# Token sums taken from the banks of the first MoE's way out, over its features as 0, 2, 1, 3

## The chip, the cores and the metric

The kernel runs on one NeuronCore of a Trainium2 chip. The metric is the time of one execution in microseconds of the device. The core's engines are TensorE (PE in the rows, its weight loads PEld), VectorE (DVE), ScalarE (ACT), GpSimd (POOL) and SyncE (SP), which here only issues DMAs. TensorE has two levels of its clock, 1.2 and 2.4 GHz; a granted clock of 1.00 in the rows is the higher.

## The reference, cut to what matters

```python
def reference(**kwargs):
    attn_out = _attn_ref(q, k, v, proj)              # (2, 8, 768, 64), masked by hash buckets
    x = attn_out.transpose(0, 2, 1, 3).reshape(1536, 512)
    # first MoE: d_model 512, d_ff 768
    h = np.maximum(np.maximum(x @ w1, x @ w2), x @ w3)
    x = h @ w_out
    # second MoE: d_model 512, d_ff 2048
    h = x @ w_in
    g = h * (1.0 / (1.0 + np.exp(-1.702 * h)))
    return g @ w_out
```

The weights come as 64 bit floats, all else in 32 bit. The change concerns the step from `h @ w_out` of the first MoE to `x @ w_in` of the second.

## The kernel before, in words

All matrices are kept as a high part, rounded to the matmul's 32 bit format, and a low part, the rest; a product is three matmuls (high by high, high by low, low by high), each 128 by 128 by 512. Tokens lie along the free dimension, in `NCH` = 3 blocks `a` of 512; features along the partitions, in blocks of 128.

After the attention (to about 250 us) the first MoE's way in (`up1`) makes `h` in six blocks of d_ff, 54 units of 12 matmuls. Its way out (`down1`) goes over the four feature blocks `et` of 128 and the three token blocks `a`: 12 units of 18 matmuls. Each unit fills one bank of PSUM; ScalarE copies it to the high part `xh` (L641) and VectorE subtracts to get the low part `xl` (L642). This is the input `X[1]` of the second MoE.

The second MoE goes over the 2048 features of d_ff in eight rounds `p` of two blocks of 128 (`FG` = 2). In round 0 the way in is plain: six units `up2` of 12 matmuls (two feature blocks by three token blocks). From round 1 on the products of the two feature blocks with the first two token blocks are taken with seven products instead of eight (`seven`, a form of Strassen's scheme, on 2 by 2 blocks): each is 6 matmuls, and they need sums of weight blocks (`sums`: `shi`, `slo`, made by GpSimd and ScalarE from round to round) and four sums of token blocks T1 to T4 (`ts[0]` to `ts[3]`, tiles `th` and `tl`, made once). The third token block goes plain, in two units `up2`. The way out (`down2`) has 12 units of 6 matmuls a round, which are added up in `res`.

The token sums use blocks numbered by feature half and token block: for `c` = 0, 1 the block 11 is feature block `c` with tokens 0, 12 feature block `c` with tokens 1, 21 and 22 the same of feature block `c + 2`. T1 = 12 - 11, T2 = 22 - T1, T3 = 22 - 12, T4 = T2 - 21. `token_sums()` returns 16 steps. Each block is put together as `xh + xl` on VectorE (L689), subtracted on VectorE (L702), the result copied to the high part on ScalarE (`high`, L693) and subtracted to the low part (`low`, L696) on GpSimd (T1, T2) or VectorE (T3, T4). One step is issued after each unit of round 0: six in `up2`, ten in `down2`.

What fixes the order: `unit` calls a unit's function, then the work that the unit before put into `due` (so gelu's second half comes one unit late), then `after`, then `w_tick`, which lets every weight block in flight take its next step. Every engine goes through its instructions in the order in which they are issued (`in_order`). A weight block's steps are: raw load (two buffers, the next load is issued after L468), magnitude on ScalarE (L448), clamp on GpSimd (L452), three bit steps on VectorE (L460, L464, L468), cast to `whi` on ScalarE and `wlo` on GpSimd (L475, L495). gelu is a sigmoid on ScalarE (L666), a product on VectorE (L669), and the split `gh` and `gl` on ScalarE and GpSimd (L670, L671).

The memory pools lie on top of each other: `mo[0]` for the whole MoE part, `mo[2]` above it, first with the `h` of the first MoE (`sb_h`), then with what the second needs (`sb_g`). The banks are eight tiles `acc`.

Of the kernel before, what the change touches and what calls it, by code (L numbers as in the profile page):

```python
# [6 lines left out]
F32R = mybir.dt.float32r  # L7
# [4 lines left out]
ALU = mybir.AluOpType  # L12

P = 128
CH = 512
# [75 lines left out]
def build(tc, q, k, v, proj, w1, w2, w3, w_out, m2_in, m2_out, out):  # L91
    nc = tc.nc
# [5 lines left out]
    EC = E // P  # L98
# [18 lines left out]
    def st(shape, tag, bufs, dtype=F32, pool=None):  # L117
        seq[0] += 1
        if pool is None:
            pool = sb if tag in shared else at  # L120
        return pool.tile(shape, dtype, tag=tag, name=f"{tag}_{seq[0]}", bufs=bufs)
# [12 lines left out]
    def f32(ap):  # L134
        return ap.bitcast(F32)
# [163 lines left out]
    X = {}  # L299
# [100 lines left out]
    def w_block(key, src, n, tag):  # L400
        wplace[key] = len(wblocks)
        wblocks.append((src, n, tag))

    def w_out_group(n):
        for f in range(n * FG, (n + 1) * FG):
            w_block(("out", f), m2_out[f * P:(f + 1) * P, :].rearrange("p (c f) -> p c f", c=EC), EC, "wo")
# [2 lines left out]
        for i, w in enumerate((w1, w2, w3)):  # L409
            w_block(("up", ft, i), w[:, ft * P:(ft + 1) * P].rearrange("(c p) f -> p c f", p=P), EC, "w")  # L410
    w_out_group(0)
    for et in range(EC):
        for a in range(2):
            w_block(("down", et, a), w_out[a * 3 * P:(a + 1) * 3 * P, et * P:(et + 1) * P]
                    .rearrange("(c p) f -> p c f", p=P), 3, "w")
# [135 lines left out]
    def w_tick(start):  # L551

        for entry in list(wflight):
            i, steps = entry
            if i is not None and split_is_next(steps) and not w_free(i) or i is None and not sums_free():
                break
            step = steps.pop(0)
            if step:
                step()
            if not steps:  # L560
                wflight.remove(entry)
        i = wstate[1]
        if start and i < len(wblocks) and len(wflight) < (5 if wstage[0] else 3) and i in wraw and (mo[0] is not None or wblocks[i][2] == "w"):
            wflight.append((i, w_steps(i)))
            wstate[1] += 1
            wflight[-1][1].pop(0)()
            return True
        return False
# [6 lines left out]
    def w_get(*key):  # L575
        i = wplace[key]
        if i not in wsplit:
            raise RuntimeError(f"block {i} is used before it is split")
        return wsplit[i]
# [6 lines left out]
    mo = [None, None, None]  # L586
# [3 lines left out]
    def bank():  # L590
        seq[0] += 1
        return mo[1].tile([P, CH], F32, tag="acc", name=f"acc_{seq[0]}", bufs=8)
# [26 lines left out]
    def split1(ft, a):  # L619
        if a == 0:  # L620
            Hs[ft] = (st([P, NTOK], "hh", FT, F32R, mo[2]), st([P, NTOK], "hl", FT, F32R, mo[2]))
        hh, hl = Hs[ft]
        s = slice(a * CH, (a + 1) * CH)
        nc.scalar.copy(hh[:, s], hm[a])
        nc.gpsimd.tensor_tensor(out=hl[:, s], in0=hm[a], in1=f32(hh[:, s]), op=ALU.subtract)

    def down1(et, a):
        cur = [w_get("down", et, n) for n in range(2)]
        if not X.get(1):
            X[1] = (st([P, EC, NTOK], "xh", 1, F32R), st([P, EC, NTOK], "xl", 1, F32R))  # L630
        xh, xl = X[1]
        s = slice(a * CH, (a + 1) * CH)
        o = bank()
        for c in range(FT):
            (wh, wl), (hh, hl) = cur[c // 3], Hs[c]
            for z, (w, h) in enumerate(((wh, hh), (wh, hl), (wl, hh))):
                nc.tensor.matmul(o, w[:, c % 3, :], h[:, s], start=(c == 0 and z == 0),  # L637
                                 stop=(c == FT - 1 and z == 2))
        if a == NCH - 1:
            wdone.update(wplace["down", et, n] for n in range(2))  # L640
        nc.scalar.copy(xh[:, et, s], o)  # L641
        nc.vector.tensor_tensor(out=xl[:, et, s], in0=o, in1=f32(xh[:, et, s]), op=ALU.subtract)  # L642


    gs = {}
# [30 lines left out]
    ts = {}  # L676
    due = []

    def token_sums():

        xh, xl = X[1]
        steps = []
        for n in range(4):
            ts[n] = tuple(st([P, 2, CH], f"t{z}{n}", 1, F32R, mo[2]) for z in "hl")

        def block(c, half, a):
            t = st([P, CH], "hc", 4, pool=mo[0])
            s = slice(a * CH, (a + 1) * CH)
            nc.vector.tensor_tensor(out=t, in0=f32(xh[:, c + 2 * half, s]), in1=f32(xl[:, c + 2 * half, s]), op=ALU.add)  # L689
            return t  # L690

        def high(n, c, t):
            nc.scalar.copy(ts[n][0][:, c], t)  # L693

        def low(n, c, t, eng):
            eng.tensor_tensor(out=ts[n][1][:, c], in0=t, in1=f32(ts[n][0][:, c]), op=ALU.subtract)  # L696

        for c in range(2):
            got = {}

            def sub(to, x, y):
                nc.vector.tensor_tensor(out=to, in0=x, in1=y, op=ALU.subtract)  # L702

            def a(c=c, got=got):
                got["11"], got["12"] = block(c, 0, 0), block(c, 0, 1)

            def b(c=c, got=got):
                sub(got["11"], got["12"], got["11"])
                got["22"] = block(c, 1, 1)

            def d(c=c, got=got):
                high(0, c, got["11"])
                sub(got["12"], got["22"], got["12"])

            def e(c=c, got=got):
                low(0, c, got["11"], nc.gpsimd)
                high(2, c, got["12"])
                sub(got["22"], got["22"], got["11"])

            def f(c=c, got=got):  # L720
                low(2, c, got["12"], nc.vector)
                high(1, c, got["22"])
                got["21"] = block(c, 1, 0)

            def g(c=c, got=got):
                low(1, c, got["22"], nc.gpsimd)
                sub(got["21"], got["22"], got["21"])

            def h(c=c, got=got):
                high(3, c, got["21"])  # L730

            def i(c=c, got=got):
                low(3, c, got["21"], nc.vector)
            steps += [a, b, d, e, f, g, h, i]
        return steps

    def seven(p):

# [96 lines left out]
    if True:  # L835
# [89 lines left out]
        for j in range(2):  # L925
            for n in range(8):
                bits = n > 3
                name, a = "kq"[n // 2 % 2], n % 2
# [23 lines left out]
        for u in range(NU):  # L952
            hd, c = divmod(u, NTILE)
            g, j = divmod(hd, 2)
# [12 lines left out]
        for jq in range(NU // 2):  # L967
            hd, i = divmod(jq, 3)
            g, j = divmod(hd, 2)
# [55 lines left out]
        def unit(fn, *args, after=None, matmuls=12, target=None):  # L1025
            n = len(due)
            fn(*args)
            for _ in range(n):
                due.pop(0)()
            if after:  # L1030
                after()
            if target is not None:
                w_tick(wstate[1] < target)
                return
            owed[0] = min(owed[0] + matmuls / 12, 2 * PACE)
            for _ in range(2 if matmuls > 12 else 1):
                if w_tick(owed[0] >= PACE and wstate[1] < wplace["in", FG]):
                    owed[0] -= PACE
# [4 lines left out]
        for ft in range(1, FT):  # L1043
            for i in range(3):
                for a in range(NCH):
                    unit(up1, ft, i, a, bank, after=(lambda: split1(ft, a)) if i == 2 else None)
        for et in range(EC):
            for a in range(NCH):
                unit(down1, et, a, matmuls=3 * FT)
        sb_h.__exit__(None, None, None)  # L1050
        sb_g = tc.tile_pool(name="sb_g", bufs=1, reuse_waits="tile")
        mo[2] = sb_g.__enter__()
        steps = token_sums()
        wstage[0] = True

        def ahead():
            if steps:
                steps.pop(0)()

        for p in range(FT2 // FG):  # L1060

            nxt = wplace.get(("in", FG * (p + 1)), len(wblocks))
            if p == 0:
                for n in range(NCH * FG):
                    unit(up2, n % FG, n // FG, after=ahead, target=nxt + 1 + (n >= 2))
                    w_tick(False)
            else:
                while steps:
                    steps.pop(0)()
                for n, x in enumerate(seven(p)):  # L1070
                    unit(x, matmuls=6, target=nxt + 1 + (n >= 4))
                for f in range(FG):
                    unit(up2, FG * p + f, NCH - 1, target=nxt + 2)
            for t in range(B * NTILE):
                unit(down2, p, t, matmuls=6, after=ahead, target=nxt + 2 + (t >= 1) + (t >= 6))
# [34 lines left out]
```

## Time and profile before

| | us |
|---|---|
| time, median of 3 runs (lowest to highest) | 703.24 (702.67 to 703.45) |
| the profiled execution | 702.86 |
| its span, from the first to the last instruction | 701.1 |
| TensorE busy | 690.2 (98%) |
| VectorE busy | 535.1 (76%) |
| GpSimd busy | 452.3 (65%) |
| ScalarE busy | 372.0 (53%) |
| mean granted clock of TensorE | 0.995 |

Times in the rows count from the span's start. A matmul's duration in the rows reaches from its start to its modelled end and overlaps the next one, so the distance between starts is what it takes of the engine. Brackets behind an instruction show its engine's idle time before it and what ended it; `L` and a number is the line in the kernel.

### The profile page before, as it was taken

The numbers are of one execution on the slowest core, as the hardware profiler recorded it, in microseconds if no ns is written. First come the engines' busy times: TensorE is split into PE (matmuls) and PEld (weight loads), VectorE is DVE, ScalarE is ACT, GpSimd is POOL, SyncE is SP. The second block draws the span as 40 slices with busy tenths as digits, with TensorE's granted clock in tenths as the row PEclk, the third lists the DMA queues.
The fourth block names the chain that finished last, engine by engine and source line by source line (L and its number), as shares of the span: only waits on it lengthen the run. The fifth ranks groups of instructions, "written<-read, shape, count | busy, mean of one in ns | idle before, by whom it ended". The sixth has DMA issues, their size and how long they took to land.

```text
span 701.1 us, 10931 instructions
## 1 busy us (share of the span) xinstructions
PE 690.2 (98%) x3741; PEld 591.4 (84%) x3742; DVE 535.1 (76%) x928; ACT 372.0 (53%) x727; POOL 452.3 (65%) x488
## 2 busy tenths in 40 slices
PE   9999999999999999999999999997999999999998
PEld 5899999999999988888888888885888888888886
DVE  7999999999999736634555353889888878798864
ACT  4898898888889713332323222654443534344340
POOL 5487878798888844524543422585959687785950
PEclk9999999999999999999999999998999999999999
DMA  5657676777454103321212122002221121212104
GB/s 115 142 133 158 132 181 145 174 175 166 110 130 107 49 6 97 111 64 60 90 47 75 38 80 64 31 30 61 73 74 64 62 87 64 61 61 60 61 0 180
DMA packets 74406, 63.34 MB, mean 90 GB/s; under 512 B 41376, under 2 KB 65184, under 8 KB 74352
## 3 DMA queue, kind: packets, MB, share of 16 engines
q1 hardware_dynamic: 74128, 62.52, 34.2%
q8 instruction: 30, 0.49, 0.3%
q14 instruction: 24, 0.20, 0.1%
q10 hardware_dynamic: 224, 0.13, 0.1%
HBM read 38.80 MB, written 3.15 MB: 60 GB/s over the span
## 4 chain that ended last, share of the span: by engine, by line
PE 89%; DVE 6%; POOL 2%; issue 1%; DMA 1%; ACT 0%; SPq 0%; DVEq 0%; POOLq 0%; ACTq 0%
PE acc L604 20%; PE acc L814 16%; PE acc L790 9%; PE S L307 8%; PE PV L355 8%; PE T L337 8%; PE acc L637 7%; PE acc L655 6%; PE T L205 2%; PE T L178 1%; DVE se L314 1%; DVE ptl L347 1%; PE T L604 1%; DVE hc L702 1%; POOL wlo L495 0%
## 5 line engine op out<-in xcount | busy, mean ns | idle before, releaser
L671 POOL TENSOR_TENSOR gl<-hm,gh 128x512 fp32r<-128x512 f32 x48 | 74.4, 1573 | 49.7 <-ACT gh L670 49.7
L328 POOL TENSOR_SCALAR se<-se,rc 128x768 f32<-128x768 f32 x96 | 87.5, 924 | 24.3 <-DVE rc L325 8.9
L347 DVE TENSOR_TENSOR ptl<-T,pth 128x512 fp32r<-128x512 f32 x144 | 94.5, 682 | 3.6 <-ACT pth L343 3.5
L320 ACT ACTIVATE se<-se,mn 128x768 f32<-128x768 f32 x96 | 90.9, 947 | 5.3 <-DVE se L314 4.7
L314 DVE TENSOR_SCALAR_CACHE_REDUCE se<-S 128x768 f32<-128x768 f32 x96 | 90.9, 949 | 1.9 <-PE S L307 1.6
L307 PE MATMUL S<-kst,qst 128*128 128x512 f32 (+3 forms) x384 | 87.0, 350 | 0.0
L343 ACT CAST pth<-T 128x512 fp32r<-128x512 f32 x144 | 80.2, 588 | 12.6 <-PE T L337 10.6
L337 PE MATMUL T<-ident,se 128*128 128x128 f32 x576 | 80.4, 273 | 0.8 <-DVE ptl L347 0.6
L604 PE MATMUL acc<-xh,whi 128*128 128x512 f32 x204 | 79.4, 389 | 0.0
L604 PE MATMUL acc<-xl,whi 128*128 128x512 f32 x204 | 79.4, 389 | 0.0
L604 PE MATMUL acc<-xh,wlo 128*128 128x512 f32 x204 | 79.4, 389 | 0.0
L819 DVE TENSOR_TENSOR res<-acc,res 128x512 f32<-128x512 f32 (+1 forms) x85 | 57.3, 679 | 24.7 <-PE acc L814 24.5
L814 PE MATMUL acc<-wolo,gh 128*128 128x512 f32 (+1 forms) x194 | 75.0, 387 | 0.0
L814 PE MATMUL acc<-wohi,gh 128*128 128x512 f32 (+1 forms) x194 | 74.9, 387 | 0.0
L495 POOL TENSOR_TENSOR wlo<-wmag,whi 128x512 fp32r<-128x512 f32 (+1 forms) x42 | 56.6, 1348 | 28.3 <-ACT whi L475 28.3
L355 PE MATMUL PV<-pth,vst 128*128 128x256 f32 x288 | 74.5, 293 | 0.0
L448 ACT ACTIVATE wbits<-wraw 128x512 f32<-128x512 f32 (+1 forms) x58 | 37.9, 656 | 66.5 <-DMA wraw<-in_moe_w_dram 29.9
L452 POOL TENSOR_SCALAR wbits<-wbits 128x512 f32<-128x512 f32 (+1 forms) x58 | 40.4, 696 | 49.0 <-ACT wbits L448 48.6
L337 PEld LDWEIGHTS T<-ident,se 128*128 128x128 f32 x576 | 65.4, 140 | 5.9 <-DVE ptl L347 1.1
L355 PE MATMUL PV<-ptl,vst 128*128 128x256 f32 x288 | 70.2, 279 | 0.0
L614 DVE TENSOR_TENSOR hm<-acc,hm 128x512 f32<-128x512 f32 x34 | 23.5, 690 | 56.8 <-PE acc L604 54.5
L307 PEld LDWEIGHTS S<-kst,qst 76*128 76x128 f32 (+1 forms) x384 | 59.2, 190 | 5.3 <-DVE se L314 0.5
(159 smaller groups left out, 1635.3 us busy)
## 6 DMA issues: line engine op xcount, KB each, us to landing
wraw<-in_moe_w_dram SPq DMA_DIRECT2D x18, 512.0 KB
wraw<-in_moe_w_out_dram SPq DMA_DIRECT2D x16, 512.0 KB
wraw<-in_moe_w_in_dram SPq DMA_DIRECT2D x16, 512.0 KB
kst<-kq SPq DMA_DIRECT2D x42, 192.0 KB
qst<-kq SPq DMA_DIRECT2D x42, 192.0 KB
raw<-in_k_dram SPq DMA_DIRECT2D x16, 192.0 KB
raw<-in_q_dram SPq DMA_DIRECT2D x16, 192.0 KB
raw<-in_v_dram SPq DMA_DIRECT2D x16, 192.0 KB
```

Of the source, the lines that this page charges most:

```text
L307: nc.tensor.matmul(pss[:, x], qs[r, k, c * P:(c + 1) * P], ks[r, k, x], start=k == 0, stop=k == 1)
L314: nc.vector.tensor_scalar(out=se[u], in0=pss[:, :S], scalar1=1.0e9, scalar2=None, op0=ALU.min, op1=ALU.min, accum_out=mn[u])
L320: nc.scalar.activation(se[u], se[u], AF.Exp, bias=mn[u], scale=-1.0, accum_out=sm[u // 2][:, u % 2:u % 2 + 1])
L328: nc.gpsimd.tensor_scalar(out=se[u], in0=se[u], scalar1=rc[u // 2][:, u % 2:u % 2 + 1], scalar2=1.0, op0=ALU.mult, op1=ALU.mult)
L337: nc.tensor.transpose(pst[:, i * P:(i + 1) * P], se[2 * jq + o][:, c * P:(c + 1) * P], ident)
L343: nc.scalar.copy(ptr[jq][0][:, n * 512:(n + 1) * 512], tps[jq, n])
L347: nc.vector.tensor_tensor(out=ptr[jq][1][:, s], in0=tps[jq, n], in1=f32(ptr[jq][0][:, s]), op=ALU.subtract)
L355: nc.tensor.matmul(pv[jq], vs[:, c, :], ptr[jq][t].rearrange("p (o c n) -> p c o n", o=2, c=NTILE)[:, c], start=(c == 0 and t == 0), stop= ...
L604: nc.tensor.matmul(o, w[:, c, :], x[:, c, s], start=(c == 0 and z == 0), stop=(c == EC - 1 and z == 2))
L671: nc.gpsimd.tensor_tensor(out=gl, in0=g, in1=f32(gh), op=ALU.subtract)
L790: nc.tensor.matmul(o, w[:, c], x[:, c], start=n == 0, stop=n == len(turns) - 1)
L814: nc.tensor.matmul(o, g[:, s], w.rearrange("p c f -> p (c f)")[:, e], start=n == 0, stop=n == len(turns) - 1)
```

## The change

The way out goes over the feature blocks as 0, 2, 1, 3, and the weight blocks are listed in the same order. So the four blocks of `c` = 0 are done in its first half and those of `c` = 1 in its second. Each unit of `down1` now calls `token_sums(c, half, a, o)` with its bank `o`: the blocks 11 and 21 are copied out of the bank by ScalarE, T1 and T2 are subtractions of VectorE that read the bank, and one unit later (`rest`, in `due`) T3 and T4 follow as subtractions between tiles, and T1 and T3 are split. T2 and T4 are split in 8 steps that are issued after the units of round 0, one each. All low parts are made on GpSimd. The tiles of T1 and T3 are in `mo[0]`, those of T2 and T4 in `mo[2]`; two of the unsplit sums take the tag `hm0`, the others `hc`. The sums come from the bank's values instead of `xh + xl`.

```diff
--- before.py
+++ after.py
@@ -409,7 +409,9 @@
         for i, w in enumerate((w1, w2, w3)):
             w_block(("up", ft, i), w[:, ft * P:(ft + 1) * P].rearrange("(c p) f -> p c f", p=P), EC, "w")
     w_out_group(0)
-    for et in range(EC):
+
+    ETS = [c + half * EC // 2 for c in range(EC // 2) for half in range(2)]
+    for et in ETS:
         for a in range(2):
             w_block(("down", et, a), w_out[a * 3 * P:(a + 1) * 3 * P, et * P:(et + 1) * P]
                     .rearrange("(c p) f -> p c f", p=P), 3, "w")
@@ -640,6 +642,7 @@
             wdone.update(wplace["down", et, n] for n in range(2))
         nc.scalar.copy(xh[:, et, s], o)
         nc.vector.tensor_tensor(out=xl[:, et, s], in0=o, in1=f32(xh[:, et, s]), op=ALU.subtract)
+        due.append(token_sums(et % 2, et // 2, a, o))
 
 
     gs = {}
@@ -676,63 +679,44 @@
     ts = {}
     due = []
 
-    def token_sums():
-
-        xh, xl = X[1]
-        steps = []
-        for n in range(4):
-            ts[n] = tuple(st([P, 2, CH], f"t{z}{n}", 1, F32R, mo[2]) for z in "hl")
-
-        def block(c, half, a):
-            t = st([P, CH], "hc", 4, pool=mo[0])
-            s = slice(a * CH, (a + 1) * CH)
-            nc.vector.tensor_tensor(out=t, in0=f32(xh[:, c + 2 * half, s]), in1=f32(xl[:, c + 2 * half, s]), op=ALU.add)
-            return t
-
-        def high(n, c, t):
-            nc.scalar.copy(ts[n][0][:, c], t)
-
-        def low(n, c, t, eng):
-            eng.tensor_tensor(out=ts[n][1][:, c], in0=t, in1=f32(ts[n][0][:, c]), op=ALU.subtract)
-
-        for c in range(2):
-            got = {}
-
-            def sub(to, x, y):
-                nc.vector.tensor_tensor(out=to, in0=x, in1=y, op=ALU.subtract)
-
-            def a(c=c, got=got):
-                got["11"], got["12"] = block(c, 0, 0), block(c, 0, 1)
-
-            def b(c=c, got=got):
-                sub(got["11"], got["12"], got["11"])
-                got["22"] = block(c, 1, 1)
-
-            def d(c=c, got=got):
-                high(0, c, got["11"])
-                sub(got["12"], got["22"], got["12"])
-
-            def e(c=c, got=got):
-                low(0, c, got["11"], nc.gpsimd)
-                high(2, c, got["12"])
-                sub(got["22"], got["22"], got["11"])
-
-            def f(c=c, got=got):
-                low(2, c, got["12"], nc.vector)
-                high(1, c, got["22"])
-                got["21"] = block(c, 1, 0)
-
-            def g(c=c, got=got):
-                low(1, c, got["22"], nc.gpsimd)
-                sub(got["21"], got["22"], got["21"])
-
-            def h(c=c, got=got):
-                high(3, c, got["21"])
-
-            def i(c=c, got=got):
-                low(3, c, got["21"], nc.vector)
-            steps += [a, b, d, e, f, g, h, i]
-        return steps
+    td = {}
+
+    def t_high(n, c, t, pool):
+        if n not in ts:
+            ts[n] = tuple(st([P, 2, CH], f"t{z}{n}", 1, F32R, pool) for z in "hl")
+        nc.scalar.copy(ts[n][0][:, c], t)
+
+    def t_low(n, c, t):
+        nc.gpsimd.tensor_tensor(out=ts[n][1][:, c], in0=t, in1=f32(ts[n][0][:, c]), op=ALU.subtract)
+
+    def token_sums(c, half, a, o):
+
+
+        if (half, a) == (0, 0):
+            td[c, "11"] = st([P, CH], "hc", 4, pool=mo[0])
+            nc.scalar.copy(td[c, "11"], o)
+        elif (half, a) == (0, 1):
+            td[c, 0] = st([P, CH], "hc", 4, pool=mo[0])
+            nc.vector.tensor_tensor(out=td[c, 0], in0=o, in1=td[c, "11"], op=ALU.subtract)
+        elif (half, a) == (1, 0):
+            td[c, 3] = st([P, CH], "hm0", 2)
+            nc.scalar.copy(td[c, 3], o)
+        elif (half, a) == (1, 1):
+            td[c, 1] = st([P, CH], "hc", 4, pool=mo[0])
+            nc.vector.tensor_tensor(out=td[c, 1], in0=o, in1=td[c, 0], op=ALU.subtract)
+
+        def rest():
+            if (half, a) == (0, 1):
+                t_high(0, c, td[c, 0], mo[0])
+            elif (half, a) == (1, 0):
+                t_low(0, c, td[c, 0])
+            elif (half, a) == (1, 1):
+                nc.vector.tensor_tensor(out=td[c, "11"], in0=td[c, 1], in1=td[c, "11"], op=ALU.subtract)
+                nc.vector.tensor_tensor(out=td[c, 3], in0=td[c, 1], in1=td[c, 3], op=ALU.subtract)
+            elif (half, a) == (1, 2):
+                t_high(2, c, td[c, "11"], mo[0])
+                t_low(2, c, td[c, "11"])
+        return rest
 
     def seven(p):
 
@@ -1044,14 +1028,15 @@
             for i in range(3):
                 for a in range(NCH):
                     unit(up1, ft, i, a, bank, after=(lambda: split1(ft, a)) if i == 2 else None)
-        for et in range(EC):
+        for et in ETS:
             for a in range(NCH):
                 unit(down1, et, a, matmuls=3 * FT)
         sb_h.__exit__(None, None, None)
         sb_g = tc.tile_pool(name="sb_g", bufs=1, reuse_waits="tile")
         mo[2] = sb_g.__enter__()
-        steps = token_sums()
         wstage[0] = True
+        steps = [f for c in range(2) for n in (1, 3) for f in ((lambda c=c, n=n: t_high(n, c, td[c, n], mo[2])),
+                                                               (lambda c=c, n=n: t_low(n, c, td[c, n])))]
 
         def ahead():
             if steps:
@@ -1065,8 +1050,6 @@
                     unit(up2, n % FG, n // FG, after=ahead, target=nxt + 1 + (n >= 2))
                     w_tick(False)
             else:
-                while steps:
-                    steps.pop(0)()
                 for n, x in enumerate(seven(p)):
                     unit(x, matmuls=6, target=nxt + 1 + (n >= 4))
                 for f in range(FG):
```

## Rows read from the trace of the kernel before

**Rows 1.** Chain of waits from 389 us on: start, length (us), what.

```profile
389.62 48.96 PE acc L637 x216
...
478.57 0.63 ACT th L693
...
509.92 9.52 PE acc L790 x42
519.44 5.44 PE acc L655 x24
```

**Rows 2.** TensorE's timeline, 438 to 488 us: start, length, line, operation.

```profile
438.42 0.39 PE L655 MATMUL acc<-xh,whi 128*128 128x512 f32 x1
...
471.06 0.39 PE L790 MATMUL acc<-xh,whi 128*128 128x512 f32 x1
...
473.78 0.39 PE L790 MATMUL acc<-th,whi 128*128 128x512 f32 x1
474.00 0.39 PE L790 MATMUL acc<-tl,whi 128*128 128x512 f32 x1
479.24 0.80 PE L790 MATMUL acc<-th,whi 128*128 128x512 f32 x1 [4.85 <-ACT th L693]
...
488.00 0.39 PE L655 MATMUL acc<-xh,whi 128*128 128x512 f32 x1
```

**Rows 3.** Busy time of the engines in three stretches.

```profile
389.62:438.58 48.96, 48.96 (x218) 40.54 (x217) 21.54 (x30) 12.27 (x23) 11.97 (x14) 1.00 0.20 60
438.58:471.06 32.48, 32.48 (x145) 26.87 (x144) 27.42 (x30) 18.50 (x33) 22.70 (x18) 1.00 0.10 33
471.06:488.00 16.94, 12.09 (x44) 9.22 (x42) 15.91 (x17) 8.90 (x17) 11.16 (x9) 0.80 0.22 63
```

**Rows 4.** VectorE's timeline, end of the token sums.

```profile
470.96 1.51 DVE L460 TENSOR_SCALAR wmag<-wbits 128x512 uint32<-128x512 uint32 x1 [1.77 <-POOL wbits L452]
...
477.44 1.09 DVE L702 TENSOR_TENSOR hc<-hc,hc 128x512 f32<-128x512 f32 x1
```

**Rows 5.** VectorE's groups by shape, 389.62 to 480 us.

```profile
L689 DVE TENSOR_TENSOR hc<-xh,xl 128x512 f32<-128x512 f32 x8 | 10.6, 1345 | 0.0
L702 DVE TENSOR_TENSOR hc<-hc,hc 128x512 f32<-128x512 f32 x8 | 8.8, 1096 | 0.1
L642 DVE TENSOR_TENSOR xl<-acc,xh 128x512 fp32r<-128x512 f32 x12 | 8.3, 692 | 27.6 <-ACT xh L641 27.6
```

**Rows 6.** Instructions of line 696: ns shortest/median/longest.

```profile
L696 DVE TENSOR_TENSOR tl<-hc,th x4: 691/1170/1783, 451.4 to 479.2; 128x512 fp32r<-128x512 f32 x4
L696 POOL TENSOR_TENSOR tl<-hc,th x4: 1288/1499/1743, 452.0 to 475.3; 128x512 fp32r<-128x512 f32 x4
```

**Rows 7.** ScalarE's groups by shape, 389.62 to 480 us.

```profile
L641 ACT CAST xh<-acc 128x512 fp32r<-128x512 f32 x12 | 7.0, 585 | 20.8 <-PE acc L637 20.8
...
L693 ACT CAST th<-hc 128x512 fp32r<-128x512 f32 x8 | 5.0, 624 | 4.7 <-DVE hc L702 4.7
```

**Rows 8.** Timelines of VectorE, ScalarE, GpSimd: weights of the last down block.

```profile
415.37 1.08 DVE L460 TENSOR_SCALAR wmag<-wbits 128x384 uint32<-128x384 uint32 x1
...
417.07 0.56 DVE L468 SCALAR_TENSOR_TENSOR wmag<-wraw,wmag 128x384 uint32<-128x384 uint32 x1
...
421.48 0.66 ACT L448 ACTIVATE wbits<-wraw 128x512 f32<-128x512 f32 x1 [6.34 <-DMA wraw<-in_moe_w_in_dram]
...
422.51 0.52 ACT L475 CAST whi<-wmag 128x384 fp32r<-128x384 f32 x1
...
423.10 1.01 POOL L495 TENSOR_TENSOR wlo<-wmag,whi 128x384 fp32r<-128x384 f32 x1 [6.87 <-ACT whi L475]
```

**Rows 9.** GpSimd's timeline, 457 to 476 us.

```profile
457.79 1.63 POOL L671 TENSOR_TENSOR gl<-hm,gh 128x512 fp32r<-128x512 f32 x1 [2.35 <-ACT gh L670]
...
462.33 1.74 POOL L671 TENSOR_TENSOR gl<-hm,gh 128x512 fp32r<-128x512 f32 x1
...
472.15 3.15 POOL L542 TENSOR_TENSOR slo<-hm,shi 128x512 fp32r<-128x512 f32 x2
```

## The prediction

> **What bounds the kernel now.** Read the chain of waits first, then TensorE's own timeline where the chain changes engine, then the other engines' timelines backward from there. In the chain the matmuls follow each other without a gap from the first MoE's way out on: 216 of them in 48.96 us; later, for one pair of features, seven products with 42 in 9.52 us and an up part with 24 in 5.44 us [rows 1]. So a matmul in step costs 9.52 / 42 = 0.2267 us, whatever duration the profile gives the single one. On such a stretch the other engines cost nothing, unless TensorE has to wait for them.
>
> It waits once. In the first round of seven products the third ("22" by "T4") does its first two matmuls and stops: the second starts at 474.00, the next was due at 474.23 and starts at 479.24 [rows 2]. That is 5.01 us of idle. The granted clock, 1.00 before, is 0.80 in the mean over the stretch [rows 3], and the matmuls behind the wait follow one another more slowly for a while. Both together by counting: from 473.78, where this product starts, to 488.00, where the next up part starts [rows 2], there are 5 products of 6, thus 30 matmuls. They take 14.22 us; in step they would take 30 x 0.2267 = 6.80. The loss is **7.42 us**: 5.01 the wait, 2.41 the slow pace.
>
> Why so late? The cast of `th` at 478.57 [rows 1] waited for VectorE's subtraction at 477.44 [rows 4]. VectorE was behind with its own queue there: from 438.58 to 471.06 it was busy 27.42 of 32.48 us [rows 3], and the token sums are 24.2 us of its work up to 480 (10.6 and 8.8 [rows 5], and four low parts, 1.2 in the mean, within the 0.691 to 1.783 of [rows 6]). At 470.96 it had also stood 1.77 us behind a weight step that waited for GpSimd [rows 4]. The block sums took 1.35 and the subtractions 1.10 in the mean, where a subtraction that reads a bank takes 0.69 [rows 5].
>
> **The change, part by part.** *Removed:* the eight block sums on VectorE (10.6 us). *Moved:* all eight subtractions, and the split into high and low of T1 and T3, go to the way out, where each of 12 units (18 matmuls, 4.08 us) leaves a bank to be read. The split of T2 and T4 stays behind, in 8 steps (four casts, four low parts), one in each of the six up units and the first two down units. All eight low parts are now GpSimd's; four were VectorE's.
>
> The way out gets: on VectorE four subtractions out of a bank at 0.69, 2.8 us, and four between tiles at 0.69 to 1.78, 2.8 to 7.1 us; busy time goes from 21.54 to between 27 and 31.5 of 48.96 us [rows 3]. ScalarE gets four copies of 0.585 and three casts of 0.624 [rows 7]: from 12.27 to 16.5. GpSimd gets three low parts at 1.29 to 1.74 [rows 6]: from 11.97 to about 16.5. None is near full, and TensorE asks them for two things only: a free bank (there are eight, so each is needed again 8 units, or 32 us, later) and split weights. The bank reads are covered; the weights are the thing to check.
>
> The tightest is the last down block's. VectorE's weight step that ends at 417.63 frees a raw tile; the load into it lands, ScalarE's magnitude step that waits for it starts at 421.48, the cast of `whi` follows at 422.51, GpSimd's `wlo` runs from 423.10 to 424.11 [rows 8]. TensorE wants this `wlo` in the tenth unit, which starts three units before the first up matmul at 438.42 [rows 2], thus at 426.18, in its twelfth matmul: 426.18 + 11 x 0.2267 = 428.67. Slack now 4.6 us. The change puts two tile subtractions ahead of VectorE's weight steps at 415.37: 1.4 us undisturbed, 3.6 at the worst duration. It puts a bank copy and a cast ahead of `whi` (0.585 + 0.624 = 1.2), and a low part ahead of `wlo`, of which the cast of `whi`, 0.52, covers some and 0.8 to 1.2 is left. So `wlo` ends between 424.11 + 1.4 + 1.2 + 0.8 = 427.5 and 424.11 + 3.6 + 1.2 + 1.2 = 430.1. I take 427.6, near the lower end, since the only GpSimd operation nearby for VectorE to meet is one `wlo`. The cost is 0, at the upper end 1.4 us. One subtraction reuses a tile that this low part reads last, so VectorE may wait for it; behind it stand a bank read and a weight step whose result is used 10 us later.
>
> The order 0, 2, 1, 3 has the same 216 matmuls, and the weight blocks are listed in that order too. Feature block 3 stays last, so the first up unit has its input as early as now. T1's and T3's tiles move to the pool below, and those above shift down; what lay there is read for the last time before their first writes. All this at 0.
>
> Behind the way out VectorE is rid of 24.2 us. T4's last low part is issued in the second down unit, which ends at 438.42 + (72 + 12) x 0.2267 = 457.5. On GpSimd it stands behind the `gl` that ended at 462.33 + 1.74 = 464.07 [rows 9]; 1.74 more makes 465.8. It is wanted at 474.23: 8 us to spare.
>
> GpSimd is the engine to look at next. From 438.58 to 471.06 it was busy 22.70 of 32.48 us [rows 3]; with five low parts there, in place of two and the start of a third, 26 to 28. What TensorE wants from it first is `slo`, the split sums of the weights: the fourth product starts at 471.06 [rows 2] + 18 x 0.2267 = 475.14 and takes `slo` in its fifth matmul, at 476.05. It ended at 472.15 + 3.15 = 475.30 [rows 9]. Between GpSimd's last idle time, before 457.79 [rows 9], and `slo`, two low parts of 1.29 ran, and two will again; the other three fall where GpSimd had idle time. So `slo` ends at 475.3 (two parts as now) to 476.2 (both at 1.74) even if nothing starts earlier. I expect about 471: the 2.35 us of idle before 457.79 hung on VectorE, and two-input operations took up to 1.74 for the 1.29 they take undisturbed.
>
> The Trainium skill (GPSIMD Engine Reference, 4.1 Engine selection) speaks against moving low parts: elementwise work with two inputs belongs on VectorE, on GpSimd it takes about twice as long. For the operation alone the trace agrees (0.691 against 1.288 at best [rows 6]); were that paid on TensorE's path, four parts at 0.6 more would take 2.4 us off the gain, 698.2.
>
> **Sum.** Nothing is added to TensorE's path, and 7.42 us of waiting and slow pace go. The profiled execution took 702.86 us (span 701.1, 1.76 around it): span 693.7, time 695.4. The median of the runs is 703.24, 0.38 higher; by it **695.8 us**. Later rounds are in step already and give nothing more.
>
> **Rivals.** *The whole stall goes* (the forecast): 695.8, own range 695.2 to 696.5. For it: by the middle values above no engine comes within 1 us of TensorE's wish, most not within 4. 78%.
>
> *A short new wait takes its place.* Either GpSimd's idle time doesn't absorb one of the earlier low parts and `slo` ends 1.29 later than its bound, 477.5, 1.4 us late; or the last `wlo` comes at its upper bound, also 1.4 late. That gives 697.2, and 698.4 if half of the slow pace comes with it. Against it: GpSimd's waits ahead of the gelu parts, which shorten when VectorE is free. 12%.
>
> *No gain:* the wait only moves on to `slo`, which was next behind T4 and 0.75 us from its due time. Held up till 481, it brings wait and slow pace back: about 703. GpSimd would have to be 5 us beyond its latest bound. 4%.
>
> *Slower:* the place is the tenth unit of the way out, the mechanism the weights' chain through VectorE, a load, ScalarE and GpSimd, now behind token work on all three. A wait of x costs x and up to 2.41 of slow pace. From x = 5.0 the gain is spent; from x = 6.4 (`wlo` at 435.1) the kernel is slower by over 1.4 us; at x = 8, 706. The bound ends 5 us short of that. 5%. The last 1% is a gain beyond the forecast.
>
> A measurement of this kernel can tell about 0.2%, 1.4 us. Faster by more: 91% (78 + 12 + 1); within: 4%; slower: 5%. The range, 694.9 to 698.6, takes in the short new waits.
>
> **What would show it.** The third matmul of the third product 0.2267 us behind the second; the clock at 1.00 and 9.52 us for the 42 matmuls of the first round; VectorE's busy time from 438 to 471 down by over 10 us, with no sum of `xh` and `xl`; four bank subtractions near 0.69 in the way out; its last `wlo` before 428.7, `slo` before 476. The prediction is wrong if TensorE waits anywhere from 389 to 488, on `wlo`, `slo` or a bank.

## The result, and the profile after

The changed kernel takes 695.36 us (median of 4 runs, 695.09 to 695.65) against 703.35 before (4 runs, 702.67 to 703.71). The ratio is 0.9886, its 95% interval 0.9873 to 0.9900. The profiled execution took 695.58 us, its span is 693.8, the mean granted clock 1.00. Forecast: 695.8 us and a span of 693.7.

In the chain of waits of the changed kernel (start, length, what) the matmuls of the second MoE now follow each other without a gap:

```profile
390.01 48.96 PE acc L639 x216
438.97 16.32 PE acc L658 x72
455.29 16.32 PE acc L798 x72
471.61 9.52 PE acc L774 x42
481.13 5.44 PE acc L658 x24
...
674.25 16.40 PE acc L798 x78
```

The first round of seven products is a piece of 42 in 9.52 us like all later rounds [rows 1]. The way out starts 0.39 us later than before; over all 14 traces of this case it starts anywhere from 388.96 to 390.06, so this is put down to no edit. Times of this trace are therefore to be read 0.39 us back when they are set beside those of before.

TensorE's timeline, changed kernel, where the wait was:

```profile
474.17 0.39 PE L774 MATMUL acc<-th,whi 128*128 128x512 f32 x1
474.40 0.39 PE L774 MATMUL acc<-tl,whi 128*128 128x512 f32 x1
474.62 0.39 PE L774 MATMUL acc<-th,whi 128*128 128x512 f32 x1
...
476.44 0.61 PE L774 MATMUL acc<-th,slo 128*128 128x512 f32 x2
...
480.97 0.39 PE L658 MATMUL acc<-xh,whi 128*128 128x512 f32 x1
```

The third matmul of the third product starts 0.22 us after the second, where it was 5.24 [rows 2]. From this product to the next up part it is 480.97 - 474.17 = 6.80 us where it was 14.22: the 7.42 us of the forecast, to the last digit. The span fell by 7.3 us: 7.42, less the 0.39 lost ahead of the way out, and 0.27 more that went behind the last matmul. The median fell by 7.99; the 0.57 above the forecast's 7.42 is within the spread of the runs (1.04 us before) and no trace puts it anywhere.

Busy time of the engines in the same three stretches of the clock, not moved by the 0.39 us (TensorE, its loads, VectorE, ScalarE, GpSimd, clock, DMA share, GB/s), changed kernel:

```profile
389.62:438.58 48.96, 48.96 (x217) 40.54 (x216) 25.02 (x36) 16.19 (x30) 16.93 (x17) 1.00 0.19 60
438.58:471.06 32.48, 32.48 (x145) 26.90 (x144) 17.39 (x18) 20.72 (x37) 26.10 (x23) 1.00 0.10 33
471.06:488.00 16.94, 16.94 (x77) 14.02 (x76) 14.86 (x20) 9.15 (x17) 9.22 (x9) 1.00 0.30 94
```

Against [rows 3]: VectorE falls from 27.42 to 17.39 us in the full stretch and rises from 21.54 to 25.02 in the way out, GpSimd rises to 26.10, and the clock of the last stretch is 1.00 instead of 0.80. With the stretches moved by 0.39 us, VectorE's figure in the full stretch is 17.78, a fall of 9.6 us instead of 10.0; the way out stays at 25.02.

One place came closer than forecast. Timelines of VectorE, ScalarE, GpSimd and TensorE of the changed kernel around the last down block's weights:

```profile
415.76 1.41 DVE L714 TENSOR_TENSOR hc<-hc,hc 128x512 f32<-128x512 f32 x1
417.09 0.68 DVE L715 TENSOR_TENSOR hm<-hc,hm 128x512 f32<-128x512 f32 x1
417.69 0.35 DVE L462 TENSOR_SCALAR wmag<-wbits 128x384 uint32<-128x384 uint32 x1
...
418.67 0.56 DVE L470 SCALAR_TENSOR_TENSOR wmag<-wraw,wmag 128x384 uint32<-128x384 uint32 x1
...
423.06 0.66 ACT L450 ACTIVATE wbits<-wraw 128x512 f32<-128x512 f32 x1 [7.54 <-DMA wraw<-in_moe_w_in_dram]
423.63 0.57 ACT L643 CAST xh<-acc 128x512 fp32r<-128x512 f32 x1
424.96 0.59 ACT L697 COPY hc<-acc 128x512 f32<-128x512 f32 x1 [0.76 <-DVE xl L644]
425.44 0.62 ACT L687 CAST th<-hc 128x512 fp32r<-128x512 f32 x1
425.96 0.52 ACT L477 CAST whi<-wmag 128x384 fp32r<-128x384 f32 x1
...
427.40 1.01 POOL L497 TENSOR_TENSOR wlo<-wmag,whi 128x384 fp32r<-128x384 f32 x1
...
429.06 0.39 PE L639 MATMUL acc<-hh,wlo 128*128 128x512 f32 x1
```

`wlo` ends at 428.41 and TensorE takes it at 429.06: 0.65 us to spare, where before there were 4.6. This time to spare is called the room from here on.

GpSimd's timeline, changed kernel, the last low part of T4 and the split sums of the weights:

```profile
463.08 1.29 POOL L690 TENSOR_TENSOR tl<-hm,th 128x512 fp32r<-128x512 f32 x1
...
467.68 2.74 POOL L544 TENSOR_TENSOR slo<-hm,shi 128x512 fp32r<-128x512 f32 x2
```

### The profile page after: what moved, and what is told of

The parts are those of the page before. It is cut to its first block, busy times and chain, and to the rows that moved or that the text cites. A ratio compares the mean times of both kernels' runs of the same rounds, so it can differ in the third digit from the quotient of the medians.

```text
span 693.8 us, 10926 instructions
## 1 busy us (share of the span) xinstructions
PE 687.2 (99%) x3741; PEld 590.0 (85%) x3742; DVE 521.4 (75%) x916; ACT 374.2 (54%) x731; POOL 454.7 (66%) x492
## 3 DMA queue, kind: packets, MB, share of 16 engines
HBM read 38.80 MB, written 3.15 MB: 60 GB/s over the span
## 4 chain that ended last, share of the span: by engine, by line
PE 95%; DVE 3%; DMA 1%; issue 1%; POOL 0%; SPq 0%; DVEq 0%; POOLq 0%
PE acc L606 20%; PE acc L798 19%; PE acc L774 10%; PE S L307 9%; PE T L337 9%; PE PV L355 8%; PE acc L658 8%; PE acc L639 7%; PE T L205 2%; PE T L178 1%; PE T L606 1%; DVE ptl L347 1%; DVE se L314 1%; DMA raw<-in_v_dram 0%; DMA pf<-in_proj_dram 0%
```

## The experiments

All are compared with the kernel before, run on the same chip (its median was 702.95 to 703.48 us there, 703.35 with the result); "no wait" means that TensorE's list of waits is empty from 300 us on.

**The order alone (e1).** The kernel before, with two lines changed:

```diff
-    for et in range(EC):
+    ETS = (0, 2, 1, 3)
+    for et in ETS:
...
-        for et in range(EC):
+        for et in ETS:
             for a in range(NCH):
                 unit(down1, et, a, matmuls=3 * FT)
```

> The kernel before with only the order of the feature blocks changed to 0, 2, 1, 3. My theory (the gain is the one wait for T4 and the slow matmuls behind it, and the order only makes the early sums possible): no change, 703.2 to 703.5 us, and the third product still waits about 5 us. Rival (the order itself gains, through the weight loads or an earlier input of the second MoE): below 702.

702.61 us, ratio 0.9991 (0.9981 to 1.0000). TensorE's waits from 300 us on (who waited for whom: total, times, longest) are those of before:

```profile
PE acc L791 <- ACT th L694: 4.8, 1, 4.8
```

The time lies 0.6 us under the range that was expected and over the rival's 702. By its interval the order gains at most 0.2%, and it leaves the wait as it was.

**The banks without the order (e2).** The changed kernel with the old order:

```diff
-    ETS = [c + half * EC // 2 for c in range(EC // 2) for half in range(2)]
+    ETS = (0, 1, 2, 3)
...
-            td[c, "11"] = st([P, CH], "hc", 4, pool=mo[0])
+            td[c, "11"] = hm_tile()
```

> The changed kernel with the old order 0, 1, 2, 3; two unsplit blocks lie in a tile of gelu's instead, since four blocks have to be held longer. My theory: the sums are done by the end of the way out either way, T4 is in time, 695.4 us, and the last down block's low part comes about 2 us earlier than in the changed kernel, as fewer token steps stand ahead of it. Rival (the order is needed for the time): a wait for T4 or in the way out, 697 or more.

694.99 us, ratio 0.9885 (0.9866 to 0.9904), no wait. Three of the four runs lie between 694.51 and 695.02, the fourth at 697.47, within what the rival allowed; it was not profiled, and what it waited for is open. By the median and the trace the order isn't needed for the time. It saves tiles: in the old order two more are held at once than the tag `hc` has, and this kernel takes them from gelu's. But the new order costs room at the last down block's weights. GpSimd's timeline of this kernel:

```profile
423.99 1.01 POOL L497 TENSOR_TENSOR wlo<-wmag,whi 128x384 fp32r<-128x384 f32 x1 [7.90 <-ACT whi L477]
```

The last down block's `wlo` ends at 425.0, in a trace that lies 1.05 us ahead of the changed kernel's (way out from 388.96), so TensorE takes it at 428.0: 3.0 us of room instead of 0.65.

**The place without the banks (e4).** The changed kernel, with every block put together from its two parts on VectorE again:

```diff
+        et, s = c + 2 * half, slice(a * CH, (a + 1) * CH)
+
+        def block(t):
+            nc.vector.tensor_tensor(out=t, in0=f32(X[1][0][:, et, s]), in1=f32(X[1][1][:, et, s]), op=ALU.add)
...
-            nc.scalar.copy(td[c, "11"], o)
+            block(td[c, "11"])
...
-            nc.vector.tensor_tensor(out=td[c, 0], in0=o, in1=td[c, "11"], op=ALU.subtract)
+            block(td[c, 0])
+            nc.vector.tensor_tensor(out=td[c, 0], in0=td[c, 0], in1=td[c, "11"], op=ALU.subtract)
```

and the same for `td[c, 3]` and `td[c, 1]`.

> The changed kernel, but each block is put together again as high plus low part on VectorE, at the same places of the way out, instead of being read from the bank. My theory (what counts is that the work leaves VectorE's full stretch of round 0, not that the block sums are saved): the gain stays, 695.4 to 696.0 us, with VectorE's busy time in the way out up by about 6 us. Rival (reading the banks is the gain): the last weights of the way out come late or T4 does, 698 or more.

695.17 us, ratio 0.9881 (0.9866 to 0.9895), no wait. Busy time in the way out, this kernel:

```profile
389.60:438.50 48.90, 48.90 (x217) 40.49 (x216) 31.62 (x44) 14.41 (x27) 17.56 (x16) 1.00 0.19 60
```

This kernel's way out lies 0.9 us earlier than the changed kernel's; in its own stretch, 389.11 to 438.07, VectorE is busy 32.07 us. That is some 7 us more than the 25.02 of the changed kernel, and it costs nothing. So what gains is *when* the work is done; that the block sums fall away is a saving off the path.

**Earlier in the queue, but in the same stretch (e8).** The kernel before:

```diff
         def ahead():
-            if steps:
-                steps.pop(0)()
+            for _ in range(2):
+                if steps:
+                    steps.pop(0)()
```

> The kernel before, with two token steps issued after each unit of round 0 instead of one: the same work, earlier in the queue. My theory (VectorE has not the time for it in round 0): the wait moves from T4 to the last gelu parts of round 0, whose VectorE product now stands behind nearly all token work and would come near 471, with its low part near 474, while the way out wants it at 466.8: a wait of some 5 to 8 us, 700 to 706 us. Rival (T4 was only issued too late): 695.8 us.

704.8 us, ratio 1.0026 (1.0012 to 1.0039). The waits of TensorE, this kernel:

```profile
PE acc L814 <- POOL gl L671: 3.0, 2, 2.3
PE acc L814 <- ACT gh L670: 1.7, 1, 1.7
PE acc L814 <- ACT res L817: 0.3, 1, 0.3
```

T4 is in time, and the waits stand at gelu's parts instead, 4.7 us (0.3 more is for a bank), near the low end of what was expected. The trace is of a run of 703.73; the ten runs go up to 706.86. The longest of these waits, 2.3 us for `gl`, came through GpSimd, which in the chain of waits works from 463.03 to 469.81 without a gap. The two engines had not the time in this stretch; asking earlier only chooses who comes late.

**The low parts on GpSimd alone (e9).** The kernel before:

```diff
-                low(2, c, got["12"], nc.vector)
+                low(2, c, got["12"], nc.gpsimd)
...
-                low(3, c, got["21"], nc.vector)
+                low(3, c, got["21"], nc.gpsimd)
```

> The kernel before with all eight low parts on GpSimd, and nothing else of the change. My theory: VectorE is relieved of 4.8 us, but GpSimd has no 6 us to spare before the sums of weights, so the wait moves from VectorE to GpSimd and stays some 3 to 6 us long: 700 to 704 us. Rival (the move of the low parts is what gained): 697 or less.

704.33 us, ratio 1.0015 (1.0006 to 1.0025): the waits for T4 add up to 6.1 us instead of 4.8. The waits, then a line of VectorE's timeline:

```profile
PE acc L790 <- ACT th L693: 4.2, 1, 4.2
PE acc L790 <- POOL tl L696: 1.9, 1, 1.9
...
471.57 1.52 DVE L460 TENSOR_SCALAR wmag<-wbits 128x512 uint32<-128x512 uint32 x1 [3.15 <-POOL wbits L452]
```

The wait for `th`, which comes through VectorE's subtraction, is only 0.6 us shorter, although VectorE has four low parts less to do: it stood 3.15 us behind a weight step of GpSimd, where before it was 1.77 [rows 4]. Behind `th` stands a low part on GpSimd, which has no time of its own.

**The low parts back on VectorE (e5).** The changed kernel:

```diff
     def t_low(n, c, t):
-        nc.gpsimd.tensor_tensor(out=ts[n][1][:, c], in0=t, in1=f32(ts[n][0][:, c]), op=ALU.subtract)
+        (nc.vector if n in (1, 3) else nc.gpsimd).tensor_tensor(out=ts[n][1][:, c], in0=t, in1=f32(ts[n][0][:, c]), op=ALU.subtract)
```

> The changed kernel with the four low parts of T2 and T4 on VectorE instead of GpSimd. My theory (both engines have time to spare in round 0 now): 695.4 us, no different; GpSimd's last sums of weights end some 2 to 4 us earlier. Rival (GpSimd, about twice as slow at such an operation, sits on the path): faster than 695 by 1 us or more.

695.23 us, ratio 0.9890 (0.9875 to 0.9905), no wait. GpSimd's timeline of this kernel, whose trace lies 0.47 us ahead of the changed kernel's:

```profile
465.04 2.74 POOL L544 TENSOR_TENSOR slo<-hm,shi 128x512 fp32r<-128x512 f32 x2
```

`slo` ends at 467.78, against 470.42 there: 2.2 us earlier when the traces are set beside each other, and TensorE waits for it in neither.

**The copy ahead of the low part (e7).** The changed kernel, with `token_sums` of the units that copy (`a` = 0) called between `xh` and `xl`:

```diff
         nc.scalar.copy(xh[:, et, s], o)
+        then = token_sums(et % 2, et // 2, a, o) if a == 0 else None
         nc.vector.tensor_tensor(out=xl[:, et, s], in0=o, in1=f32(xh[:, et, s]), op=ALU.subtract)
-        due.append(token_sums(et % 2, et // 2, a, o))
+        due.append(then or token_sums(et % 2, et // 2, a, o))
```

> The changed kernel with ScalarE's copy of a block out of the bank issued ahead of VectorE's low part instead of behind it. In the trace of the changed kernel these copies wait 0.76 us for VectorE, which reads the same bank. My theory: the copy no longer waits, the low part of the last down block ends near 427.7 instead of 428.4, and the time stays 695.4, as TensorE did not wait for it. Rival (the narrow place costs something already): 0.5 us or more faster.

695.24 us, ratio 0.9893 (0.9876 to 0.9909), no wait. ScalarE's timeline, then VectorE's and GpSimd's, this kernel:

```profile
423.15 0.57 ACT L643 CAST xh<-acc 128x512 fp32r<-128x512 f32 x1
423.62 0.59 ACT L698 COPY hc<-acc 128x512 f32<-128x512 f32 x1
...
424.24 0.69 DVE L645 TENSOR_TENSOR xl<-acc,xh 128x512 fp32r<-128x512 f32 x1 [3.75 <-ACT hc L698]
...
426.05 1.01 POOL L497 TENSOR_TENSOR wlo<-wmag,whi 128x384 fp32r<-128x384 f32 x1
```

Now the copy follows the cast at once, and VectorE waits for the copy. `wlo` ends at 427.06 in a trace that lies 0.52 us ahead, so 427.6 on the changed kernel's scale, 0.8 us earlier.

**Delay at the narrow place (e10, e6, e11).** The changed kernel with 2, 4 and 10 repeats of a subtraction, ahead of VectorE's weight steps in the sixth unit of the way out; the repeats write the same values again (here with 2):

```diff
                 nc.vector.tensor_tensor(out=td[c, 3], in0=td[c, 1], in1=td[c, 3], op=ALU.subtract)
+                for _ in range(2 if c == 0 else 0):
+                    nc.vector.tensor_tensor(out=td[c, 1], in0=o, in1=td[c, 0], op=ALU.subtract)
```

> The changed kernel with two repeats of the bank subtraction at the same place as the four of the run before, 1.4 us by its trace (four took 2.87). If the room before the last down block's low part is the 0.65 us of the changed kernel's trace and the load behind it lands as fast as there (3.8 us): 0.8 us of waiting, 696.2 us. If the load lands later, as in the run with four (5.2 us): 2.2 us of waiting and some slow pace, up to 699. No room lost at all (rival): 695.3.

> The changed kernel with four repeats of a bank subtraction (same operands, same result) on VectorE, ahead of the weight steps of the sixth unit of the way out: 4 x 0.6 = 2.4 us more. In the changed kernel the low part of the last down block ends 0.65 us before TensorE wants it. My theory: it now comes 1.75 us late, a wait of that length in the tenth unit, 697.1 us, up to 2.4 more if the clock falls. Rival (there is more room than the rows say): 695.4.

> The same with ten repeats, 7.2 us. My theory puts TensorE's wait at 6.5 us (7.2 less 0.65), 8 with a late load, plus about 2 of slow pace: 703.5 to 705.5 us, so the change's whole gain is lost by this one place. Rival (the wait is taken up elsewhere, by the banks or the first up units): below 702.

| repeats | their time, us | time of the kernel, us (all runs) | ratio to before (interval) | TensorE's waits, us |
|---|---|---|---|---|
| none | 0 | 695.36 (695.09 to 695.65) | 0.9886 (0.9873 to 0.9900) | none |
| 2 | 1.42 | 696.09 (695.70 to 696.50) | 0.9906 (0.9892 to 0.9921) | 0.7 |
| 4 | 2.87 | 700.43 (697.61 to 702.41) | 0.9964 (0.9949 to 0.9978) | 3.2 |
| 10 | 7.22 | 703.88 (702.89 to 704.72) | 1.0013 (1.0004 to 1.0022) | 5.8 |

The matmuls that take this `wlo`, with two and with ten repeats:

```profile
429.95 0.50 PE L639 MATMUL acc<-hh,wlo 128*128 128x512 f32 x1 [0.67 <-POOL wlo L497]
...
434.98 0.80 PE L639 MATMUL acc<-hh,wlo 128*128 128x512 f32 x1 [0.80 <-POOL wlo L497]
```

Counted by matmuls in step from the last one ahead of the wait, they start 0.83 and 6.63 us late, where 0.8 and 6.5 were worked out from the 0.65 us of room; the times, 696.2 and 703.5 to 705.5, came out too. The list of waits shows less (0.7 and 5.8), since it counts idle time alone. Ten repeats also show what a wait does beyond itself: the way out took 58.1 us (389.30 to 447.38) instead of 48.96, 9.1 more for 5.8 of idle time, and the granted clock behind the wait is at the lower of its two levels. Busy time and clock (the third figure from the right) of this kernel:

```profile
436.00:440.00 4.00, 4.00 (x11) 3.13 (x10) 3.04 (x3) 0.89 (x3) 1.73 (x1) 0.50 0.07 12
```

Four repeats cost more than worked out (697.1, up to 2.4 more). The waits and ScalarE's timeline of that kernel:

```profile
PE acc L639 <- ACT whi L477: 2.0, 1, 2.0
PE acc L639 <- POOL wlo L497: 1.2, 1, 1.2
...
427.06 0.66 ACT L450 ACTIVATE wbits<-wraw 128x512 f32<-128x512 f32 x1 [11.82 <-DMA wraw<-in_moe_w_in_dram]
```

The load that ScalarE waits for had been issued at 421.91, 5.15 us before; in the changed kernel it was 3.77 (419.29 to 423.06), and in the traces with two and ten repeats 3.77 and 3.80. So 1.4 us of that wait is a load that landed late in this execution. The runs spread over 4.8 us, and only one was profiled: how much of the spread is the load and how much the clock stays open.

**The same delay where there is room (e12).** The kernel of e2, with four repeats ahead of the same weight steps:

```diff
             if (half, a) == (0, 1):
+                for _ in range(4 if c == 1 else 0):
+                    nc.vector.tensor_tensor(out=td[c, 0], in0=o, in1=td[c, "11"], op=ALU.subtract)
                 t_high(0, c, td[c, 0], mo[0])
```

> The kernel with the old order 0, 1, 2, 3 and sums from the banks, with four repeats of a bank subtraction ahead of the same weight steps of the sixth unit (2.9 us). There the last down block's low part ended 3.0 us before TensorE's wish instead of 0.65. If this room is what decides: 694.9 us when the load lands in 3.8 us, up to 1.4 us of waiting, 697, when late; well below the 700.4 of the same delay in the order 0, 2, 1, 3. Rival (the delay hurts in itself, whatever the order): 700.

694.97 us, ratio 0.9890 (0.9874 to 0.9907), no wait: the same four repeats that cost 5 us in the new order, late load included, cost nothing in the old one. They delay less there: the load behind the weight steps is issued 1.9 us later than in e2 (419.62 and 417.15, in traces 0.51 and 1.05 us ahead of the changed kernel's), where in e6 it was 2.9, and none of it landed late (3.84 us). But 1.9 is also well over the 0.65 us of the new order and under the 3.0 of the old one, so it is the room before that one tile that decides.

**GpSimd's room (e3).** The changed kernel, with eight repeats of a low part ahead of the first weights' sums:

```diff
         def low():
+            for _ in range(8 if p == 1 else 0):
+                nc.gpsimd.tensor_tensor(out=got["s"][1][:, 0:2], in0=got["x"], in1=f32(got["s"][0][:, 0:2]), op=ALU.subtract)
             for n, t in enumerate("xy"):
```

> The changed kernel with eight repeats of a low part of the weights' sums on GpSimd ahead of the first round's own, 8 x 1.3 = 10.4 us. In the changed kernel's trace the sums end at 470.42 and the fourth product wants them at 476.44, 6.0 us later. My theory (GpSimd has that much room and no more): a wait of about 4.4 us in the fourth product and up to 2.4 of slow pace, 699.8 to 702.2 us. Rivals: nothing lost, 695.3 (more room than that); or some 10 us lost (no room at all, 705).

704.09 us, ratio 1.0016 (1.0007 to 1.0025): slower than the 699.8 to 702.2 expected. The waits of TensorE and GpSimd's timeline, this kernel:

```profile
PE acc L776 <- POOL slo L546: 4.0, 1, 4.0
PE acc L800 <- ACT gh L675: 1.6, 1, 1.6
PE acc L800 <- POOL gl L676: 0.7, 1, 0.7
...
467.02 11.55 POOL L543 TENSOR_TENSOR slo<-hm,shi 128x512 fp32r<-128x512 f32 x8
478.65 2.49 POOL L546 TENSOR_TENSOR slo<-hm,shi 128x512 fp32r<-128x512 f32 x2
```

The first is near the one worked out (4.4), but by two errors that nearly cancel: the repeats took 11.55 us instead of 10.4, and the fourth product needs only the first of the two operations that make `slo` (the fifth needs the second), not the end of both. So the room is about 7.5 us (11.55 less 4.0) and not 6. The other two waits were not foreseen: GpSimd's delay also held a weight step, VectorE stood 9.75 us behind it, and gelu's first product of the round came late for the way out. Going beyond the room costs more than the first wait shows.

## Why the prediction was right

*The size of the loss.* Counted by matmuls it was 7.42 us, and 7.42 came back. That the median came 0.44 us under the 695.8 was not forecast; it is within the runs' spread. Counting took the idle time and the slow pace together; the list of waits alone shows 4.8 and would have missed a third of it.

*What causes it.* The prediction put the wait down to VectorE's queue in round 0. The chain of waits of the kernel before shows that it was two queues: through VectorE to 457, then through GpSimd almost without a gap until 470.94, then through VectorE again.

```profile
457.79 1.63 POOL gl L671
...
470.34 0.60 POOL wbits L452
...
472.39 1.78 DVE tl L696
474.18 1.68 DVE hc L689
```

The prediction names GpSimd's part only as 1.77 us that VectorE stood behind it. How the wait divides between the two no run shows, as none relieved GpSimd alone. That the token work in this stretch is the cause is shown from both sides: the same work in the way out gains all of it, even with the block sums kept (e4); the same work earlier in the same stretch gains nothing (e8); and handing four of VectorE's low parts to GpSimd without moving the rest gains nothing (e9), as VectorE then stands behind GpSimd's weight step for longer.

*The order at no cost or gain.* Right for the time (e1, e2). What was missed is that it narrows the room at the last down block's weights, because in this order four more token steps lie just ahead of them (e2: 3.0 us of room against 0.65).

*The narrow place.* The chain was right, and its room is the smallest of those worked out here, but `wlo` came 3.9 us later than before (428.41 less the 0.39 of shift, against 424.11 [rows 8]), where 3.5 was taken. The term that was too small is ScalarE's: 1.2 us for a copy and a cast, measured 1.9, since the copy first waited 0.76 for VectorE's low part, which reads the same bank. VectorE's term, 1.4 taken, came out at 1.2, with some luck: one of the two subtractions took 1.41 us beside GpSimd's `wlo`, but the weight step behind them then took 0.35 where it had been 1.08. e7 shows that turning copy and low part round moves the wait to VectorE: in neither trace do they read the bank at once. The Trainium skill (PSUM — Partial Sum Buffer, PSUM bank collisions raise a hardware error) states that two engines must not access one bank at the same time, two readers included, and that software has to keep them apart. The trace agrees with its being kept; what would happen otherwise no run here shows.

*The slower rival.* Its mechanism exists, at the place named. The prediction let the gain be spent at a wait of 5.0 us; with ten repeats 5.8 us of waiting (6.6 by counting) took all of it and 0.9 more (703.88 against the 702.99 of the kernel before on that chip). What kept the change clear of a first wait there is 0.65 us, less than the prediction's 1.1 (428.67 less 427.6). With a load in this chain that landed 1.4 us late in one of 14 traces, that no run of the result shows a wait is in part luck.

*GpSimd.* `slo` was expected near 471 and ended at 470.42; T4's last low part, with 465.8 as its bound, at 464.4. The prediction set the end of both `slo` operations against the fourth product, which takes only the first; so `slo` had some 2.1 us in the kernel before and not 0.75, and the rival *No gain* stood further off than was said. The Trainium skill (GPSIMD Engine Reference, 4.1 Engine selection) would have kept two-input work on VectorE. The kernel before bears it out (e9: slower by 0.15%), the changed one does not (e5: no difference), where TensorE waits for neither engine.

*Busy times.* VectorE in the way out was put at 27 to 31.5 us and is 25.0: the last two tile subtractions fall behind it, only one of the other two ran beside GpSimd (1.41 us, the other 0.68), VectorE's weight steps took some 0.8 us less in sum, and neighbouring instructions overlap. ScalarE and GpSimd came out at 16.2 and 16.9 for 16.5 each.

## What to carry to other kernels

When TensorE waits for a tile, look at how full the queue of the engine that makes it is over the whole stretch before, and move work to a stretch where that engine has idle time: issuing it earlier in the full stretch only picks another victim. Before moving, find the tile with the least room in the stretch that receives the work, follow its chain through every engine and load, and add what is put ahead of each link, waits between readers of one bank among them. Of two placements that time the same, take the one with more room there: e2 and e7 time as the changed kernel does by their medians and stand 3.0 and 1.5 us clear.

## What the runs showed of the hardware that was not expected

The same load of a raw weight block took 5.15 us from issue to use in one trace (e6) and 3.74 to 3.93 in the 13 others. Why it was late there is open. In that execution a room of less than 1.4 us in this chain would have been lost.

In the four traces counted here a wait of TensorE cost more than its idle time. The way out grew by 1.0 us for 0.7 of idle time (e10), by 5.4 for 3.2 (e6) and by 9.1 for 5.8 (e11); the first round of the kernel before grew by 7.42 for 4.85. With ten repeats the granted clock was 0.50 from 436 to 440; with two it was 1.00 from 428 to 434, around the wait. By the medians the costs are 0.7 (e10), 5.1 (e6) and 8.5 us (e11), set against the 695.36 of another session.
